# Top-k attention with a highway layer: earlier small top-eights, a reduction of its own for row maxima, one exponential a pair

## The chip, the cores and the metric

The kernel runs on one core of a Trainium2 chip. The metric is the device time of one execution in microseconds. TensorE (PE) does matmuls into PSUM, VectorE (DVE) and ScalarE (ACT) read PSUM and SBUF, GpSimd (POOL) works on SBUF, and the queues of SyncE (SP), ScalarE and GpSimd issue DMAs. Each engine takes its instructions in the order in which they were written; between engines, semaphores order the work.

## The reference

Attention over 8 batches, 8 heads, 576 rows and a head width of 64 keeps the 32 largest scores of each row; then a highway layer runs over the 4608 x 512 result.

```
scores = scale * np.matmul(q, k.transpose(0, 1, 3, 2))
kth = np.partition(scores, -top_k, axis=-1)[..., -top_k:-top_k + 1]
scores = np.where(scores >= kth, scores, -1000000000.0)
scores = scores - np.max(scores, axis=-1, keepdims=True)
attn = np.exp(scores)
attn = attn / (np.sum(attn, axis=-1, keepdims=True) + 1e-09)
attn_out = np.matmul(attn, v)
...
H = np.maximum(x @ w_h, 0.0)
T = 1.0 / (1.0 + np.exp(-(x @ w_t + b_t)))
out = T * H + (1.0 - T) * x
```

## The kernel before

A unit is 128 rows of scores with 576 columns. For the first 512 rows of a batch a unit is one head and one of four row tiles; the last 64 rows (the remainder) of two heads share a unit. Units go in 144 pairs, 18 a batch: 16 of whole row tiles (two heads of the same rows) and 2 of remainders. A pair's scores fill three banks of PSUM: the first unit has columns 0 to 511 in bank 0 and its last 64 at the start of bank 1, the second has its first 64 at the end of bank 1 and the rest in bank 2. Two such tiles exist (`xs`), so the scores of pair i + 2 can begin when pair i is read for the last time.

The order of all work is written by hand, in `step(i)`; 143 steps and `begin` and `finish` make the program. For pair i + 1 a step does the search for the threshold, for pair i the rest:

- PE adds the masks of pair i to its scores (`mask_add`, line 411), multiplies the weights of pair i - 3 by the values (line 501), runs filler matmuls (`spare`, line 279), then the scores of pair i + 2 (lines 310 and 319, for remainders 327 and 336), then a piece of the highway layer (line 529) or a transpose of later inputs.
- VectorE finds the eight largest of each of six segments of 96 columns of both units of pair i + 1 (`segments`, line 354, twelve instructions), then the eight largest scores below the threshold of pair i (`below`, line 424). Then comes `refine(i + 1)`: it merges the segments' eights (lines 367 to 377) and combines them (line 379, written into column 1 of the candidates). Line 383 reduces columns 0 and 1 of the candidates to each row's maximum and its threshold (the 24th or so largest score). In between stand `hits` and `pick_b` (lines 430 and 443), which pick the exact 32nd largest of pair i, and, in some steps, a reciprocal for the softmax's denominators (line 566). Last, `keep_both` (line 463) takes the minimum of the exponentials and of a 0-or-huge mask of pair i - 1. It is split in two, the first 64 columns of each unit before line 383 and the rest behind it, where no reciprocal stands in the step and both units are done alike; else it is one instruction or, in a few steps, two of another form (lines 457 and 466).
- ScalarE makes the mask of pair i - 1 (`above`, line 446), an evacuation of an earlier piece, the exponential of the first unit of pair i (`expo`, line 416), the copy of both units' scores of pair i + 1 into SBUF (line 349), perhaps another evacuation, the exponential of the second unit, and the sign masks of pair i + 1 with their counts (line 398), which wait for line 383.
- GpSimd compares the second unit with its threshold (line 449), does the additions and multiplications of the highway layer (lines 571, 617, 618, 631), `pick_a` (line 440) and `biases` (line 392), and issues DMAs. `biases` is made to wait for the last minimum.

Each row has its own maximum, taken off in the exponential through its bias. `wall` holds, for each unit, the maximum, the list that begins with the threshold, and the 32nd largest score. SP transposes the kept weights by DMA for the values' matmuls.

`finish` ends the last two pairs, checks that the search was exact for all rows (`sure`, line 948; a slow loop repeats the work otherwise) and stores the last rows.

Of the kernel before, what the change touches and what calls it, by code (L numbers as in the profile page):

```python
# [26 lines left out]
def kernel(  # L27
# [71 lines left out]
    TOP, THR, KTH = 0, 1, NPK + 1  # L99
    wall = consts.tile([P, NU + 2, NPK + 2], FP32)  # L100
    fac = consts.tile([P, 2, 2], FP32)
    nc.vector.memset(fac[:, :, 0], -scale)
    nc.vector.memset(fac[:, :, 1], -BIGK * (1.0 - 2.0**-24))
    be = consts.tile([P, NG + 1, 2, 2], FP32)
# [7 lines left out]
    eps = consts.tile([P, H], FP32)  # L112
    nc.vector.memset(eps[:], 2.0e-9)
    nc.vector.memset(wall[:, 0:2, KTH : KTH + 1], 0.0)

    def kth(u):
        return wall[:, u + 2, KTH : KTH + 1]

    def tb(u):
        return be[:, u // 2, u % 2, 0:1]  # L120

    def eb(u):
        return be[:, u // 2 + 1, u % 2, 1:2]

    cands = []
    for i in range(4):
        cand = consts.tile([P, 2, 8, 8], FP32, name=f"cand{i}")
        nc.vector.memset(cand[:, :, NSEG:, 0:1], -3.0e38)
        cands.append(cand)
# [167 lines left out]
    def scores(pair, prep):  # L297
# [5 lines left out]
        MB = 2 * BANK  # L303
        RA, RB = BANK, 2 * BANK - rem
        if qt < nfull:
            hp = heads2[0][0] // 2
            for n0 in range(0, MAIN, 256):
                for s, mo in ((0, 0), (1, MB)):
                    r = s * D
                    nc.tensor.matmul(  # L310
# [6 lines left out]
                    )  # L317
            ends = ps[:, BANK:MB].rearrange("p (a n) -> p a n", n=rem)[:, 0 :: BANK // rem - 1, :]
            nc.tensor.matmul(  # L319
                ends, qT[:, hp, qs : qs + P], kd[:, hp, :], start=True, stop=True  # L320
            )
        else:
            for (mo, ro), hh in zip(((0, RA), (MB, RB)), heads2):
                hp = hh[0] // 2
                for n0 in range(0, MAIN, 256):
                    for r in (0, D):
                        nc.tensor.matmul(  # L327
# [6 lines left out]
                        )  # L334
                for r in (0, D):
                    nc.tensor.matmul(  # L336
# [6 lines left out]
                    )  # L343
        both = bass.AP(tensor=ps.tensor, offset=ps[:].offset, ap=[ps[:].ap[0], [3 * BANK - S, 2], [1, S]])
        return ps[:, 0:S], ps[:, 3 * BANK - S : 3 * BANK], both

    def copy_scores(both):
        sc = scpool.tile([P, 2, S], FP32, name="sc")
        nc.scalar.copy(sc[:], both)  # L349
        return [sc[:, s, :] for s in range(2)]  # L350

    def segments(cand, sc, lo, hi):
        for s in range(lo, hi):
            nc.vector.max(cand[:, s, :], sc[:, s * SEG : (s + 1) * SEG])  # L354
# [4 lines left out]
    def refine(g, cand):  # L359
        u0, u1 = pairs[g][0], pairs[g][1] + 1  # L360
# [15 lines left out]
        for s in range(2):  # L376
# [6 lines left out]
        nc.vector.tensor_reduce(  # L383
            wall[:, u0:u1, TOP : THR + 1],
            cand[:, :, :, 0:2].rearrange("p s r k -> p s k r"),
            mybir.AxisListType.X,
            ALU.max,
        )
        yield

    def biases(g):
        return nc.gpsimd.tensor_tensor(be[:, g], wall[:, 2 * g : 2 * g + 2, TOP : KTH + 1 : KTH - TOP], fac[:], ALU.mult)  # L392

    def mask_count(u, ps):
# [5 lines left out]
            bias=wall[:, u, THR : THR + 1],  # L402
# [15 lines left out]

    def pair_tile(name):
# [3 lines left out]
    def below(u, ps):  # L423
        nc.vector.max(wall[:, u, THR + 1 : KTH], ps)  # L424
# [13 lines left out]
    def pick_a(pair, hit):  # L438
        u0, u1 = pair[0], pair[1] + 1
        nc.gpsimd.tensor_tensor(hit[:], hit[:], wall[:, u0:u1, THR:KTH], ALU.mult)  # L440

    def pick_b(pair, hit):
        nc.vector.tensor_reduce(wall[:, pair[0] + 2 : pair[0] + 4, KTH], hit[:], mybir.AxisListType.X, ALU.add)
# [15 lines left out]
    def keep_both(u, e, r, c0, c1):  # L459
# [3 lines left out]
        return nc.vector.tensor_tensor(out[:, :, c0:c1], e[:, :, c0:c1], r[:, :, c0:c1], ALU.min)  # L463
# [92 lines left out]
    def ffn_pieces(b, qt, xs):  # L556
# [4 lines left out]
        def norm():  # L561
            xs3 = xs[:, 0 : nh * DE].rearrange("p (h e) -> p h e", e=DE)
            rinv = cpool.tile([P, H], FP32, name="rinv")
            nc.gpsimd.tensor_tensor(rinv[:, 0:nh], xs3[:, :, D], eps[:, 0:nh], ALU.add)
# [18 lines left out]
            yield True  # L583
# [571 lines left out]
```

## Time and profile before

| | |
|---|---|
| median of 3 runs | 799.22 us (799.0 to 799.35) |
| the profiled execution | 800.24 us, its span 798.6 us |
| VectorE busy | 768.6 us |
| ScalarE busy | 756.8 us |
| TensorE busy | 692.5 us |
| GpSimd busy | 564.9 us |
| mean granted clock of TensorE | 0.996 |

A group line of the profile shows line, engine, operation, output and inputs with their shapes, the count, then busy time in us and the mean length of one in ns, then the idle time ahead of the group and what ended it. A timeline line shows start and length in us. A wait shows who waited for whom, the total in us, how often and the longest. A line by stretches shows the stretch, its length, and for each engine the busy time and the instructions in it, then TensorE's granted clock, the DMA engines' busy share and GB/s. In the chain's shares, an engine's name with q is its queue.

### The profile page before, as it was taken

The numbers are of one execution on the slowest core, as the hardware profiler recorded it, in microseconds if no ns is written. First come the engines' busy times: TensorE is split into PE (matmuls) and PEld (weight loads), VectorE is DVE, ScalarE is ACT, GpSimd is POOL, SyncE is SP. The second block draws the span as 40 slices with busy tenths as digits, with TensorE's granted clock in tenths as the row PEclk, the third lists the DMA queues.
The fourth block names the chain that finished last, engine by engine and source line by source line (L and its number), as shares of the span: only waits on it lengthen the run. The fifth ranks groups of instructions, "written<-read, shape, count | busy, mean of one in ns | idle before, by whom it ended". The sixth has DMA issues, their size and how long they took to land.

```text
span 798.6 us, 20350 instructions
## 1 busy us (share of the span) xinstructions
PE 692.5 (87%) x6459; PEld 494.4 (62%) x6459; DVE 768.6 (96%) x3947; ACT 756.8 (95%) x1401; POOL 564.9 (71%) x750
## 2 busy tenths in 40 slices
PE   7889998888988888888997889889898888988884
PEld 5666766666666666566665656656666666666552
DVE  6999999999999999999999999999999999999996
ACT  5999999999999999999999999999999999999984
POOL 2666867777777777787777876778777787676760
PEclk9999999999999999999999999999999999999998
DMA  6699967976799667987589766898677985565653
GB/s 123 87 132 167 133 121 138 155 130 94 137 156 151 109 97 134 157 143 117 98 147 164 125 112 111 154 149 129 109 128 141 166 117 100 96 110 100 114 85 89
DMA packets 341780, 100.32 MB, mean 126 GB/s; under 512 B 326048, under 2 KB 333856, under 8 KB 341664
## 3 DMA queue, kind: packets, MB, share of 16 engines
q1 hardware_dynamic: 286448, 79.14, 52.3%
q0 software_dynamic: 53536, 19.34, 22.4%
q8 instruction: 53, 0.87, 0.5%
q10 hardware_dynamic: 1680, 0.46, 0.3%
q14 instruction: 63, 0.52, 0.2%
HBM read 31.72 MB, written 9.44 MB: 52 GB/s over the span
## 4 chain that ended last, share of the span: by engine, by line
DVE 50%; ACT 29%; PE 14%; DMA 3%; issue 2%; SPq 1%; DVEq 0%; ACTq 0%
DVE cand L354 19%; DVE wall L424 14%; ACT m L398 8%; ACT e L416 7%; DVE ep L463 6%; ACT sc L349 6%; PE xs L327 4%; ACT r L446 3%; PE fp L529 2%; PE pso L279 2%; DMA xT<-xb 2%; PE xs L310 2%; ACT xs L515 1%; DVE en L374 1%; PE xs L411 1%
## 5 line engine op out<-in xcount | busy, mean ns | idle before, releaser
L354 DVE MAX8 cand<-xs 128x8 f32<-128x96 f32 x1728 | 298.6, 250 | 10.7 <-PE xs L336 7.0
L279 PE MATMUL pso<-cst,ident_b 128*128 128x252 bf16 x1841 | 247.0, 272 | 41.7 <-ACT xs L515 39.7
L449 POOL TENSOR_SCALAR r<-sc,wall 128x576 bf16<-128x576 f32 x135 | 232.5, 1722 | 0.0
L416 ACT ACTIVATE e<-sc,be 128x576 bf16<-128x576 f32 x288 | 227.9, 792 | 0.1
L279 PEld LDWEIGHTS <-ident_b 128*128 128x128 bf16 x1841 | 173.5, 98 | 80.7 <-issue 48.8
L424 DVE MAX8 wall<-xs 128x8 f32<-128x576 f32 x288 | 204.4, 751 | 4.5 <-PE xs L411 3.2
L310 PE MATMUL xs<-kT,qT 64*128 64x256 f32 x1024 | 145.3, 400 | 36.1 <-DVE high L367 29.7
L349 ACT COPY sc<-xs 128x1152 f32<-128x1152 f32 x144 | 161.6, 1122 | 1.0 <-DVE cand L354 0.9
L310 PEld LDWEIGHTS xs<-kT,qT 64*128 64x128 f32 x1024 | 93.1, 186 | 67.7 <-issue 40.3
L398 ACT ACTIVATE m<-xs,wall 128x576 int8<-128x576 f32 x144 | 107.9, 750 | 10.6 <-DVE wall L383 9.5
L463 DVE TENSOR_TENSOR ep<-e,r 128x1024 bf16<-128x1024 bf16 (+2 forms) x236 | 116.4, 493 | 0.3 <-issue 0.2
L440 POOL TENSOR_TENSOR hit<-hit,wall 128x18 f32<-128x18 f32 x143 | 32.2, 225 | 115.8 <-DVE hit L430 115.8
L398 ACT ACTIVATE m<-sc,wall 128x576 int8<-128x576 f32 x144 | 112.3, 780 | 0.0
L411 PE MATMUL xs<-m,ident_b 128*128 128x512 bf16 (+1 forms) x576 | 104.5, 285 | 9.0 <-ACT m L398 6.8
L446 ACT ACTIVATE r<-sc,be 128x576 bf16<-128x576 f32 x143 | 110.8, 775 | 0.0
L501 PEld LDWEIGHTS <-et 128*128 128x128 bf16 (+1 forms) x1600 | 68.6, 100 | 19.9 <-issue 3.5
L392 POOL TENSOR_TENSOR be<-wall,fac 128x4 f32<-128x4 f32 x144 | 29.1, 202 | 72.5 <-DVE ep L463 52.0
L501 PE MATMUL pso<-vb,et 128*128 128x65 bf16 (+1 forms) x1600 | 74.4, 194 | 1.1 <-DMA et<-ep 1.1
L411 PEld LDWEIGHTS <-ident_b 128*128 128x128 bf16 x576 | 51.0, 97 | 35.1 <-issue 13.8
L319 PEld LDWEIGHTS xs<-kd,qT 128*128 128x128 f32 x256 | 38.1, 188 | 42.5 <-issue 42.1
L319 PE MATMUL xs<-kd,qT 128*128 128x128 f32 x256 | 62.5, 326 | 0.0
L617 POOL TENSOR_TENSOR s<-h,x 128x512 f32<-128x512 f32 (+1 forms) x37 | 42.8, 1157 | 1.0 <-ACT h L616 1.0
(128 smaller groups left out, 999.6 us busy)
## 6 DMA issues: line engine op xcount, KB each, us to landing
kin<-in_k_dram SPq DMA_DIRECT2D x64, 128.0 KB, 3.2
qin<-in_q_dram SPq DMA_DIRECT2D x62, 128.0 KB, 3.2
out_dram<-s SPq DMA_DIRECT2D x30, 256.0 KB, 3.2
s<-h POOLq DMA_DIRECT2D x29, 256.0 KB, 3.9
xb<-x POOLq DMA_DIRECT2D x30, 128.0 KB, 2.8
vb<-in_v_dram POOLq DMA_DIRECT2D x28, 128.0 KB, 3.9
et<-ep SPq DMA_TRANSPOSE x143, 4.0
vb<-in_v_dram POOLq DMA_DIRECT2D x24, 64.0 KB, 3.1
```

The lines of the kernel that those rows point to most:

```text
L279: nc.tensor.matmul(po["t"][:, 4 * DE : BANK], ident_b[:], cst[:, 0 : BANK - 4 * DE], start=True, stop=True, skip_group_check=True,)
L310: nc.tensor.matmul(ps[:, mo + n0 : mo + n0 + 256], qT[r : r + D, hp, qs : qs + P], kT[r : r + D, hp, n0 : n0 + 256], start=(n0 == 0), stop ...
L349: nc.scalar.copy(sc[:], both)
L354: nc.vector.max(cand[:, s, :], sc[:, s * SEG : (s + 1) * SEG])
L398: nc.scalar.activation(m1[:].bitcast(I8)[:, 1 : 2 * S : 2], ps, AF.Sign, bias=wall[:, u, THR : THR + 1], scale=ABOVE, accum_out=csum[:, u ...
L411: nc.tensor.matmul(ps[:, s0:s1], ident_b[:], m1[:, s0:s1], start=False, stop=True, skip_group_check=True)
L416: nc.scalar.activation(e, sc, AF.Exp, bias=tb(u), scale=scale)
L424: nc.vector.max(wall[:, u, THR + 1 : KTH], ps)
L446: nc.scalar.activation(r, sc, AF.Relu, bias=eb(u), scale=BIGK)
L449: nc.gpsimd.tensor_scalar(r, sc, kth(u), None, ALU.is_ge)
L463: return nc.vector.tensor_tensor(out[:, :, c0:c1], e[:, :, c0:c1], r[:, :, c0:c1], ALU.min)
L501: nc.tensor.matmul(pso[r0 : r0 + ql, col : col + DE], ets[s][:, c, gi * P2 : gi * P2 + ql], vb[:, h, vc, :], start=(c == 0), stop=(c == nc ...
```

## The change

Three things are changed.

1. The matmuls of a pair's scores that write outside bank 0 are collected in `rest`, and the first unit's segments that lie wholly in bank 0 (five of six) are declared independent of them.
2. `refine` has two reductions in place of one. The first takes, over column 0 of the candidates of both units and with a padding in front and behind, the maximum of the first unit, of both units together, and of the second. The second takes the threshold of each unit from column 1.
3. For a pair of whole row tiles (128 of 144), one exponential covers both units, with the joint maximum of the pair; it stands where the first unit's stood, ahead of the score copy. The minimum of `keep_both` is always one instruction. Since the joint maximum is not each row's own, the small number added to a row's sum in the denominator is scaled: GpSimd subtracts the maxima of four pairs (`distances`) after `pick_a`, and ScalarE takes an exponential of 8 values a row (`expo_share`) in the next step, ahead of the copy of the attention output. A remainder pair keeps its two exponentials and has one more GpSimd instruction for their biases. The final check has a fourth part, that no row's maximum is too far below the joint one.

```
         for s, mo in ((0, 0), (1, MB)):
-            nc.tensor.matmul(
+            mm = nc.tensor.matmul(
...
+            if s:
+                rest.append(mm)
-    nc.tensor.matmul(ends, ...)
+    rest.append(nc.tensor.matmul(ends, ...))

-    def segments(cand, sc, lo, hi):
+    def segments(cand, sc, lo, hi, rest=()):
         for s in range(lo, hi):
-            nc.vector.max(cand[:, s, :], sc[:, s * SEG : (s + 1) * SEG])
+            ins = nc.vector.max(cand[:, s, :], sc[:, s * SEG : (s + 1) * SEG])
+            if (s + 1) * SEG <= BANK:
+                for mm in rest:
+                    tc.declare_no_dep(ins.ins, mm.ins, reason="another bank")

     # refine, behind the combination into cand[:, :, :, 1]
-        nc.vector.tensor_reduce(
-            wall[:, u0:u1, TOP : THR + 1],
-            cand[:, :, :, 0:2].rearrange("p s r k -> p s k r"),
-            mybir.AxisListType.X,
-            ALU.max,
-        )
+        at = cands4[:]
+        heads = bass.AP(tensor=at.tensor, offset=at.offset, ap=[at.ap[0], [64, 3], [64, 2], [8, NSEG]])
+        nc.vector.tensor_reduce(wall[:, g, 0:LIST], heads, mybir.AxisListType.XY, ALU.max)
+        yield
+        nc.vector.tensor_reduce(lists(g)[:, :, 0], cand[:, :, :, 1], mybir.AxisListType.X, ALU.max)
         yield

+    def biases(g):
+        if not joint(g):
+            nc.gpsimd.tensor_tensor(bs[:, g % 4], wall[:, g, 0:LIST:2], fat[:], ALU.mult)
+        return nc.gpsimd.tensor_tensor(be[:, g], wall[:, g, PEAK : KTH + LW + 1 : LW], fac[:], ALU.mult)

+    def distances(g):
+        g0 = g + 1 - NP
+        nc.gpsimd.tensor_tensor(dist[:, g0 : g + 1], wall[:, g0 : g + 1, 0:LIST:2],
+            wall[:, g0 : g + 1, PEAK].unsqueeze(2).to_broadcast([P, NP, 2]), ALU.subtract)
...
+            nc.scalar.activation(share[:], dist[...], AF.Exp, bias=eps[:, 0:1], scale=scale)

+    def exponentials(g):
+        e = pair_tile("e")
+        sc = st[g]["sc"]
+        if joint(g):
+            nc.scalar.activation(e[2][:], sc[2], AF.Exp, bias=be[:, g, 0:1], scale=scale)
+        else:
+            for s, u in enumerate(pairs[g]):
+                expo(u, sc[s], e[s])
+        return e

     # step
-            expo(pr[0], st[i]["sc"][0], st[i]["e"][0])
+            st[i]["e"] = exponentials(i)
         if nxt:
             copy_both(i + 1)
...
-            expo(pr[1], st[i]["sc"][1], st[i]["e"][1])
...
-        first = 0
-        if prev and ps_["one"] and not busy:
-            first = 64
-            keep_both(pu[0], ps_["e"][2], ps_["r"][2], 0, first)
         for _ in ra:
             pass
         last = masked()

     # finish
+        sure(3, dist[:], 1.0)
...
-        nc.vector.scalar_tensor_tensor(cond[:], wall[:, 0:NU, THR + 1], ABOVE, wall[:, 0:NU, THR], ALU.mult, ALU.add)
+        for s in range(2):
+            c = LIST + s * LW
+            nc.vector.scalar_tensor_tensor(
+                cond[:, s::2], wall[:, 0:NG, c + 1], ABOVE, wall[:, 0:NG, c], ALU.mult, ALU.add)
```

`wall` now has one row a pair, with three maxima in front of two lists, and the candidates of a pair have a column of padding on both sides; the other changes follow from that.

More of the change, by code (lines that the diff above doesn't have):

```diff
@@ L554, with denominators, ffn_pieces @@
     blocks = []
-    def ffn_pieces(b, qt, xs):
+    def denominators(e, rinv, sums, share):
+        if share is None:
+            return e.tensor_scalar(rinv, sums, 2.0e-9, None, ALU.add)
+        return e.tensor_tensor(rinv, sums, share[:], ALU.add)
+    def ffn_pieces(b, qt, xs, share=None):
         nh, ng, w = shape_of(qt)
@@ L563, in norm @@
             rinv = cpool.tile([P, H], FP32, name="rinv")
-            nc.gpsimd.tensor_tensor(rinv[:, 0:nh], xs3[:, :, D], eps[:, 0:nh], ALU.add)
+            denominators(nc.gpsimd, rinv[:, 0:nh], xs3[:, :, D], share)
             yield
@@ L651, in blk_norm @@
         rinv = cpool.tile([P, H], FP32, name="rinv")
-        nc.vector.tensor_tensor(rinv[:, 0:nh], xs3[:, :, D], eps[:, 0:nh], ALU.add)
+        denominators(nc.vector, rinv[:, 0:nh], xs3[:, :, D], k["share"])
         nc.vector.reciprocal(rinv[:, 0:nh], rinv[:, 0:nh])
```

145 lines of the change are left out of this document (92 added, 53 removed).

## The prediction

> **What bounds the kernel now.** I read the busy line of the page and the chain's shares first, then busy time in three stretches, then the waits, then VectorE's instructions in order of time.
>
> ```profile
> PE 692.5 (87%) x6459; PEld 494.4 (62%) x6459; DVE 768.6 (96%) x3947; ACT 756.8 (95%) x1401; POOL 564.9 (71%) x750
> ...
> DVE 50%; ACT 29%; PE 14%; DMA 3%; issue 2%; SPq 1%; DVEq 0%; ACTq 0%
> ```
>
> VectorE (DVE) and ScalarE (ACT) are both nearly full, and the chain changes between them and TensorE (PE). So I asked by stretch, with PE's busy time first, then its loads, VectorE, ScalarE, GpSimd:
>
> ```profile
> 378.85:388.90 10.05, 9.95 (x100) 6.94 (x101) 9.13 (x52) 9.77 (x18) 7.58 (x11) 1.00 0.59 105
> 72.00:103.00 31.00, 28.64 (x278) 21.20 (x277) 29.54 (x150) 30.22 (x57) 25.50 (x31) 1.00 0.98 133
> 399.55:430.00 30.45, 26.96 (x256) 19.29 (x253) 30.45 (x159) 29.97 (x56) 23.13 (x31) 1.00 0.86 152
> ```
>
> The third is the common case: VectorE is busy for all 30.45 us. In the second, in the first batch, ScalarE is the fuller one. The first covers the two steps of a batch whose scores are of the remainder rows (line 327): PE works 9.95 of 10.05 us, and VectorE has 0.9 us to spare. There are eight such stretches, one a batch. Which waits VectorE has:
>
> ```profile
> DVE cand L354 <- PE xs L336: 7.0, 15, 0.5
> DVE wall L424 <- PE xs L411: 3.2, 5, 1.1
> DVE cand L354 <- PE xs L319: 3.0, 7, 0.6
> PEld L529 <- DMA xT<-xb: 3.9, 4, 1.4
> PE xs L411 <- ACT m L398: 6.8, 24, 0.7
> ACT m L398 <- DVE wall L383: 9.5, 25, 0.9
> ```
>
> All that waiting is some 13 us. This is the most that better waits can return; any instruction added to VectorE costs in full wherever VectorE is the bound.
>
> **The change, part by part.**
>
> **The five small top-eights (line 354).** They will wait for the matmuls of the first bank alone; the sixth and the second unit's wait for the rest. Five of them give PE 0.8 us more, by the row of twelve in 2.07 us below, and the longest wait is 0.6, so the wait at line 354 should vanish. But who is late next? In the remainder steps (the 15 waits on line 336) the next thing VectorE needs is the mask matmuls of line 411, and they stand on PE behind the same scores, in a stretch where PE has 0.10 us of idle time. There the wait moves to line 424. I take 0.05 us a stretch, 0.4 us in all (0 to 0.8, all the idle time). The waits on line 319 are outside: 3.0 us, to which comes the overlap of 85 ns worked out below that each of the seven also loses, 3.6 in all. Behind them stands the wait for masks at line 424, so not everything counts: I take 2.8 (1.0 to 3.6).
>
> **Row maxima by their own instruction, and the joint minimum whole.** Here are a step whose minimum is split and one whose isn't, from the last combination of the refinement to the next top-eights:
>
> ```profile
> 401.77 0.19 DVE L379 SCALAR_TENSOR_TENSOR cand<-en 128x16 f32<-128x16 f32 x1
> 401.86 0.20 DVE L566 RECIPROCAL rinv<-rinv 128x8 f32<-128x8 f32 x1
> ...
> 402.00 0.21 DVE L383 TENSOR_REDUCE wall<-cand 128x4 f32<-128x32 f32 x1
> 402.12 0.75 DVE L463 TENSOR_TENSOR ep<-e,r 128x1152 bf16<-128x1152 bf16 x1
> ...
> 402.79 2.07 DVE L354 MAX8 cand<-xs 128x8 f32<-128x96 f32 x12
> ...
> 406.58 0.23 POOL L440 TENSOR_TENSOR hit<-hit,wall 128x18 f32<-128x18 f32 x1 [0.48 <-DVE hit L430]
> ...
> 406.98 0.19 DVE L379 SCALAR_TENSOR_TENSOR cand<-en 128x16 f32<-128x16 f32 x1
> 407.07 0.22 DVE L463 TENSOR_TENSOR ep<-e,r 128x128 bf16<-128x128 bf16 x1
> 407.21 0.21 DVE L383 TENSOR_REDUCE wall<-cand 128x4 f32<-128x32 f32 x1
> 407.34 0.68 DVE L463 TENSOR_TENSOR ep<-e,r 128x1024 bf16<-128x1024 bf16 x1
> ...
> 407.94 2.07 DVE L354 MAX8 cand<-xs 128x8 f32<-128x96 f32 x12
> ```
>
> ```profile
> L354 DVE MAX8 cand<-xs 128x8 f32<-128x96 f32 x1728 | 298.6, 250 | 10.7 <-PE xs L336 7.0 <-PE xs L319 3.0
> L383 DVE TENSOR_REDUCE wall<-cand 128x4 f32<-128x32 f32 x144 | 29.9, 208 | 0.2
> L443 DVE TENSOR_REDUCE wall<-hit 128x2 f32<-128x18 f32 x144 | 22.4, 156 | 0.0
> L463 DVE TENSOR_TENSOR ep<-e,r 128x128 bf16<-128x128 bf16 x101 | 22.1, 219 | 0.2 <-issue 0.2
> L566 DVE RECIPROCAL rinv<-rinv 128x8 f32<-128x8 f32 x31 | 6.1, 195 | 0.0
> L566 DVE RECIPROCAL rinv<-rinv 128x4 f32<-128x4 f32 x7 | 1.2, 170 | 0.0
> ```
>
> Instructions overlap: twelve of 250 ns would be 3.00 us and take 2.07, so each starts (3.00 - 2.07)/11 = 85 ns before the one ahead ends. From start to start, the split step spends 0.09 + 0.14 + 0.13 + 0.60 = 0.96 us here, the whole one with a reciprocal 0.09 + 0.14 + 0.12 + 0.67 = 1.02. In both the reduction starts 0.23 after the combination it depends on, whatever lies between.
>
> The new reduction of the maxima reads 36 elements, nearly what line 383 reads (32), with the same stride: 213 ns, or 0.13 from start to start. It doesn't need the combination, so it takes the place of the small minimum as filler. The second reduction reads 16 elements: between line 443 (18 dense elements, 156 ns) and line 383 (208 ns) lies 0.07 to 0.12 a start; I take 0.09, nearer to the first by size, with a little for the stride. A split step becomes 0.09 + 0.13 + 0.09 + 0.67 = 0.98, 0.025 more. A step with a reciprocal becomes 0.09 + 0.11 (195 less 85) + 0.13 + 0.09 + 0.67 = 1.09, 0.07 more.
>
> 101 steps are split and 38 (31 + 7) have a reciprocal; eight of each lie in the PE stretches, which cover the cost. 93 x 0.025 + 30 x 0.07 = 4.4 us, of which I give 0.5 back for other steps that wait at line 424 anyway: 3.9. The low end is line 443's price for both, held by the 0.23: +0.01 and nothing, 0.9 us. The high end is line 383's price for both: 0.06 and 0.11, 9 us.
>
> [...]
>
> **One exponential a pair.** ScalarE's slope and overlap:
>
> ```profile
> 400.07 0.78 ACT L416 ACTIVATE e<-sc,be 128x576 bf16<-128x576 f32 x1
> ...
> 400.74 1.11 ACT L349 COPY sc<-xs 128x1152 f32<-128x1152 f32 x1
> ```
>
> ```profile
> L416 ACT ACTIVATE e<-sc,be 128x576 bf16<-128x576 f32 x288 | 227.9, 792 | 0.1
> L349 ACT COPY sc<-xs 128x1152 f32<-128x1152 f32 x144 | 161.6, 1122 | 1.0 <-DVE cand L354 0.9
> L252 ACT COPY kT<-fp 128x512 f32<-128x512 f32 x31 | 18.2, 588 | 0.0
> ```
>
> An element costs (1122 - 588)/640 = 0.83 ns, so a joint exponential should take 792 + 576 x 0.83 = 1.27 us. Two take 1.58 less one overlap of 0.11 (0.78 - 0.67): 0.2 us less, in 128 of 144 pairs, 26 us of ScalarE's time (0 if it grew in proportion). Most of this is idle time to be: the masks wait for line 383 on VectorE 25 times already. It pays where PE waits for masks and VectorE for PE. Line 424's waits on 411 are 3.2 us, but four of its five I put down to the four late transposing DMAs before line 529, which stay. I take 1.0 (0 to 2.0), with what it adds in the first batch. The order also moves: the score copy and the evacuation after it come some 0.48 later (1.15 for the joint one against 0.67 start to start), hidden by the masks, which still come after; if that cover went, PE would wait for the evacuation before line 529.
>
> ```profile
> POOL hit L440 <- DVE hit L430: 115.8, 143, 3.7
> ```
>
> **Small additions.** 32 tiny exponentials for the denominators on ScalarE, ahead of the copy that PE's fillers wait for, 32 subtractions on GpSimd after line 440, one more check and two halves for one at the end: 0.3 us (0 to 1.5); the first are paid by the 26 us above, the subtractions fit into GpSimd's wait of 115.8 us.
>
> **The sum** against the profiled execution (800.24 us, span 798.6; 1.02 above the median of 799.22): -0.4 - 2.8 + 3.9 - 1.0 + 0.3 = 0.0. So 799.2 for the median: the waits that go pay for the instruction that comes.
>
> **The rivals.**
>
> The waits go and the reductions are cheap: line 443's price (0.9 us) and the gains near their ends (-0.8 - 3.6 - 1.5): -4.7 with the additions, 794.5. For it: VectorE's waits are real, and the filler hides in the 0.23. Against it: line 383 has the stride of both.
>
> The reductions decide, and the time is slower: with line 383's price on both (9 us, 8.5 after what is covered) and gains of 4.2 and 0.3 of additions it is 803.8. Place: between lines 379 and 463, in the stretches where VectorE is 100% busy. It decides once the two add over 0.034 us a step (4.2 / 123), which is 0.23 us for both in a split step (0.96 - 0.09 - 0.67 + 0.034). Against it: 16 elements should not cost what 32 do.
>
> GpSimd's subtraction blocks VectorE. [...]
>
> ```profile
> 281.73 1.27 POOL L617 TENSOR_TENSOR s<-h,x 128x512 f32<-128x512 f32 x1 [0.58 <-ACT h L616]
> ...
> 282.40 0.66 DVE L367 TENSOR_TENSOR high<-cand 128x48 f32<-128x48 f32 x1
> ```
>
> Line 367 took 0.66 us here for 48 elements and ended 0.06 behind GpSimd's instruction. The subtraction stands behind line 440 (406.58 to 406.81 above); at line 440's own length it would run to 407.04, and the combination starts at 406.98. If each is hit by a whole subtraction, 32 x 0.2 = 6.4 us: 805.6; the point from which it decides is the 0.06 of overlap just worked out, 1.9 us. [...]
>
> The change doesn't act: the top-eights' wait passes to line 424 everywhere and the masks come no sooner: 799.2 + 3.9 + 0.3 = 803.4, on the slower side too.
>
> **How the numbers follow.** No change is what lies within 0.2%, 1.6 us. The sum has 0.38 (its own range 797 to 801.4; a tenth of all falls below 797.6 and 0.02 above 800.8, the rest, 0.26, is no change). Cheap reductions: 0.25. Dear reductions: 0.24, a blocked VectorE 0.06, a wait that only moves 0.07. Faster 0.35, same 0.26, slower 0.39. With 794 to 804.5 the range leaves out about 2 in 10, the far ends of the cheap case and of the blocked one.
>
> **What would show it.** Line 354 has hardly any idle time before it, while line 424's wait on line 411 grows by about 0.5 us in each remainder stretch, whose length stays 10.0. The two reductions take some 213 and 172 ns. The joint exponential takes 1.27 us; ScalarE's busy share falls to about 92%, and its masks wait more often for VectorE. VectorE stays at 96% or above. It is wrong if the remainder stretches get shorter, if a reduction takes over 250 ns, or if line 379's successor or the `high` line stretches.

## The result, and the profile after

| | before | after |
|---|---|---|
| median of 20 runs each, side by side | 799.61 us (798.9 to 801.29) | 801.32 us (799.79 to 802.82) |
| ratio, 95% interval | | 1.0020 (1.0013 to 1.0026) |
| the profiled execution, its span | 800.24, 798.6 us | 801.33, 799.7 us |

The change makes the kernel 1.7 us slower. The forecast was no change, 799.2 us. The time lies within the stated range, but the interval of the ratio leaves out 1: the kernel moved, and the sum said that it would not. The changed kernel's line numbers are its own: 354 became 375, 424 became 487, 411 became 464, 383 became 410 (maxima) and 412 (thresholds), 463 became 526, 529 became 592.

The page of the changed kernel, busy times and the chain's shares:

```profile
PE 690.8 (86%) x6461; PEld 493.8 (62%) x6461; DVE 771.5 (96%) x3993; ACT 741.7 (93%) x1307; POOL 578.4 (72%) x799
...
DVE 75%; PE 13%; ACT 6%; issue 3%; DMA 2%; SPq 0%; POOL 0%; DVEq 0%; ACTq 0%; POOLq 0%
```

ScalarE is relieved by 15 us and hardly on the chain any more (29% before); VectorE has 75% of it (50% before). The program's end now hangs on VectorE, and on what makes VectorE wait. Groups of instructions, each with what ended the idle time ahead of it:

```profile
L375 DVE MAX8 cand<-xs 128x8 f32<-128x96 f32 x1728 | 298.0, 252 | 0.8 <-PE xs L328 0.7
L487 DVE MAX8 wall<-xs 128x8 f32<-128x576 f32 x288 | 205.1, 756 | 13.1 <-PE xs L464 12.0
L476 ACT ACTIVATE e<-sc,be 128x1152 bf16<-128x1152 f32 x128 | 161.0, 1257 | 0.1
```

```profile
L410 DVE TENSOR_REDUCE wall<-cand 128x3 f32<-128x36 f32 x144 | 28.6, 199 | 0.0
L436 ACT ACTIVATE share<-dist,eps 128x8 f32<-128x8 f32 x32 | 9.5, 297 | 0.0
L412 DVE TENSOR_REDUCE wall<-cand 128x2 f32<-128x16 f32 x144 | 25.9, 180 | 0.0
L622 POOL TENSOR_SCALAR rinv<-xs 128x4 f32<-128x4 f32 x7 | 1.6, 230 | 0.6
```

The idle time of 10.7 us ahead of the small top-eights is gone, and that ahead of line 487 is 13.1 where 4.5 stood: of 9.9 us taken there 8.6 turn up here, though not all for this reason, as the runs below show. In the steps of remainder rows it moved whole. Here is one of their eight stretches before (VectorE in order of time), then after:

```profile
377.38 1.41 DVE L424 MAX8 wall<-xs 128x8 f32<-128x576 f32 x2
381.07 2.08 DVE L354 MAX8 cand<-xs 128x8 f32<-128x96 f32 x12 [0.39 <-PE xs L336]
383.06 1.41 DVE L424 MAX8 wall<-xs 128x8 f32<-128x576 f32 x2
386.83 2.08 DVE L354 MAX8 cand<-xs 128x8 f32<-128x96 f32 x12 [0.54 <-PE xs L336]
389.01 1.43 DVE L424 MAX8 wall<-xs 128x8 f32<-128x576 f32 x2
```

```profile
375.71 1.42 DVE L487 MAX8 wall<-xs 128x8 f32<-128x576 f32 x2
378.96 2.06 DVE L375 MAX8 cand<-xs 128x8 f32<-128x96 f32 x12
381.35 1.43 DVE L487 MAX8 wall<-xs 128x8 f32<-128x576 f32 x2 [0.32 <-PE xs L464]
384.56 2.07 DVE L375 MAX8 cand<-xs 128x8 f32<-128x96 f32 x12
387.32 1.43 DVE L487 MAX8 wall<-xs 128x8 f32<-128x576 f32 x2 [0.69 <-PE xs L464]
```

The two steps took 389.01 - 377.38 = 11.63 us and take 387.32 - 375.71 = 11.61. The waits of 0.39 and 0.54 stand now as 0.32 and 0.69 before the masks' matmuls.

The two reductions, in a step with a reciprocal and in one without:

```profile
399.96 0.19 DVE L404 SCALAR_TENSOR_TENSOR cand<-en 128x16 f32<-128x16 f32 x1
400.05 0.20 DVE L635 RECIPROCAL rinv<-rinv 128x8 f32<-128x8 f32 x1
400.16 0.17 DVE L410 TENSOR_REDUCE wall<-cand 128x3 f32<-128x36 f32 x1
400.24 0.17 DVE L412 TENSOR_REDUCE wall<-cand 128x2 f32<-128x16 f32 x1
400.33 0.75 DVE L526 TENSOR_TENSOR ep<-e,r 128x1152 bf16<-128x1152 bf16 x1
401.00 2.07 DVE L375 MAX8 cand<-xs 128x8 f32<-128x96 f32 x12
404.08 1.43 DVE L487 MAX8 wall<-xs 128x8 f32<-128x576 f32 x2 [1.01 <-PE xs L464]
...
406.30 0.19 DVE L404 SCALAR_TENSOR_TENSOR cand<-en 128x16 f32<-128x16 f32 x1
406.39 0.21 DVE L410 TENSOR_REDUCE wall<-cand 128x3 f32<-128x36 f32 x1
406.52 0.18 DVE L412 TENSOR_REDUCE wall<-cand 128x2 f32<-128x16 f32 x1
406.62 0.75 DVE L526 TENSOR_TENSOR ep<-e,r 128x1152 bf16<-128x1152 bf16 x1
407.28 2.07 DVE L375 MAX8 cand<-xs 128x8 f32<-128x96 f32 x12
```

The step without takes 407.28 - 406.30 = 0.98 from the combination to the next top-eights (0.96 before, 0.98 forecast), the one with takes 1.04 (1.02 before, 1.09 forecast). Over all such steps of the two traces the medians are 0.986 and 0.949 without, 1.040 and 1.015 with. Between the two shown stands a wait of 1.01 us at line 487, which the kernel before did not have in this step (step 73 as counted below). What TensorE was late for there is told by the view of one tile, `xT`, which the transposing DMAs write and line 592 reads. Before, then after; the numbers behind a name are us and times:

```profile
  DMA xT<-xb: 7.1, 8
...
  PEld L529: 4.5, 5
...
DMA to landing us min/median/max: 2.4/2.8/4.8
```

```profile
  DMA xT<-xb: 9.4, 8
...
  PEld L592: 6.1, 6
...
DMA to landing us min/median/max: 2.3/2.9/5.5
```

Both kernels wait for these transfers; the changed one waits longer. Whether that is part of the change's price, and what the rest is, the runs had to tell.

### The profile page after: what moved, and what is told of

Same layout as the page of the kernel before. It is cut to its first block, busy times and chain, and to the rows that moved or that the text cites. A ratio compares the mean times of both kernels' runs of the same rounds, so it can differ in the third digit from the quotient of the medians.

```text
span 799.7 us, 20355 instructions
## 1 busy us (share of the span) xinstructions
PE 690.8 (86%) x6461; PEld 493.8 (62%) x6461; DVE 771.5 (96%) x3993; ACT 741.7 (93%) x1307; POOL 578.4 (72%) x799
## 4 chain that ended last, share of the span: by engine, by line
DVE 75%; PE 13%; ACT 6%; issue 3%; DMA 2%; SPq 0%; POOL 0%; DVEq 0%; ACTq 0%; POOLq 0%
DVE cand L375 26%; DVE wall L487 22%; DVE ep L526 9%; PE xs L345 4%; PE fp L592 3%; DVE en L399 2%; DVE en L402 2%; PE pso L296 2%; DVE cand L404 2%; DVE high L392 2%; DMA xT<-xb 2%; ACT m L451 2%; DVE low L394 2%; PE xs L464 1%; DVE neg L396 1%
## 5 line engine op out<-in xcount | busy, mean ns | idle before, releaser
L487 DVE MAX8 wall<-xs 128x8 f32<-128x576 f32 x288 | 205.1, 756 | 13.1 <-PE xs L464 12.0
L476 ACT ACTIVATE e<-sc,be 128x1152 bf16<-128x1152 f32 x128 | 161.0, 1257 | 0.1
L451 ACT ACTIVATE m<-xs,wall 128x576 int8<-128x576 f32 x144 | 107.5, 747 | 28.4 <-DVE wall L412 27.2
L464 PE MATMUL xs<-m,ident_b 128*128 128x512 bf16 (+1 forms) x576 | 102.7, 285 | 4.6 <-ACT m L451 2.8
L526 DVE TENSOR_TENSOR ep<-e,r 128x1152 bf16<-128x1152 bf16 x135 | 101.0, 748 | 0.5 <-issue 0.5
L422 POOL TENSOR_TENSOR be<-wall,fac 128x3 f32<-128x3 f32 x144 | 28.4, 197 | 66.0 <-DVE ep L526 47.7
L687 POOL TENSOR_TENSOR h<-h,x 128x512 f32<-128x512 f32 (+1 forms) x37 | 43.0, 1162 | 0.6
```

The source lines that it names most:

```text
L451: nc.scalar.activation(m1[:].bitcast(I8)[:, 1 : 2 * S : 2], ps, AF.Sign, bias=top9(u, 0, 1), scale=ABOVE, accum_out=csum[:, u : u + 1],)
L464: nc.tensor.matmul(ps[:, s0:s1], ident_b[:], m1[:, s0:s1], start=False, stop=True, skip_group_check=True)
L476: nc.scalar.activation(e[2][:], sc[2], AF.Exp, bias=be[:, g, 0:1], scale=scale)
L487: nc.vector.max(top9(u, 1), ps)
L526: return nc.vector.tensor_tensor(out, e[:], r[:], ALU.min)
```

## The experiments

Every run has the kernel before beside it, and is given as a ratio to it with its 95% interval; 0.1% is 0.8 us. Steps are counted so that step n runs from VectorE's line 424 (487) for pair n - 1 to the one for pair n.

### One part at a time, on the kernels as they are

Run e1_bank_only: the first edit alone, on the kernel before.

```
-            segments(st[g]["cand"][:, s], st[g]["ps"][s], k, k + 1)
+            segments(st[g]["cand"][:, s], st[g]["ps"][s], k, k + 1, () if s else st[g]["ps"][3])
```

> The kernel before with the first edit alone: the five small top-eights wait only for the bank they read. Theory (the removed wait mostly reappears at line 424's wait, so the edit is worth little): the idle time in front of line 354 falls from 10.7 us to under 1 us, the idle time in front of line 424 grows by 5 to 9 us, and the time is 0.5 to 2.5 us under before, 797.1 to 799.1 on a before of 799.6. Rival (the edit acts freely and the reductions eat its gain): 4 to 6 us under before. Rival (the edit does nothing): within 0.4 us of before.

797.7 us, ratio 0.9970 (0.9958 to 0.9981): 2.4 us gained. The idle time ahead of the top-eights went to 0.4 us, that ahead of the next line grew to 14.0.

Run e2_no_bank: the changed kernel without the first edit.

```
-            segments(st[g]["cand"][:, 1 + s], st[g]["ps"][s], k, k + 1, () if s else st[g]["ps"][3])
+            segments(st[g]["cand"][:, 1 + s], st[g]["ps"][s], k, k + 1)
```

> The kernel after with the first edit undone: the five small top-eights wait again for the matmuls as the tracker sets it. Theory: idle time in front of the top-eights' line comes back (5 to 10 us), the wait of the line that writes over the scores falls by 4 to 8 us, and the time is 0.5 to 2.5 us above after, 801.8 to 803.8 on an after of 801.3. Rival (the edit was worth 4 us or more and only hidden by the reductions): 805 or more. Rival (without its wait VectorE only runs into GpSimd's hold and into later transfers, so the edit loses): 800.3 or less.

804.35 us, ratio 1.0049 (1.0036 to 1.0062), 2.3 us above the changed kernel by the ratios, 3.0 by the medians. The first edit is worth about the same in both. So the loss comes from the other two.

Run e3_share_behind: the small exponential behind the copy of the attention output.

```
-        while lows:
-            lows.pop(0)()
         if back:
             back_pv(j)
             back_xs(j)
             st.pop(j)
+        while lows:
+            lows.pop(0)()
```

> The kernel after with the remainder's exponential issued behind ScalarE's copy of the output instead of ahead of it. Theory (the exponential ahead of the copy delays TensorE's filler work and the masks behind it): the steps that carry it, three of them at 0.14 us more than before, go back, and the time falls by 0.3 to 1.0 us, to 800.3 to 801.0 on an after of 801.3. Rival (it lies beside other work): within 0.3 us of after. Rival (the remainder's subtraction on GpSimd now gets its operand later and holds the steps behind it): above after by 0.5 us or more.

801.95 us, ratio 1.0023 (1.0014 to 1.0031): no gain to be seen. In the trace the three steps did go back from 5.32 to 5.18 us; the runs spread from 799.97 to 802.98, and 0.4 us drowns in that. The theory held in the step and could not be told in the time.

Run e4_two_reductions: on the kernel before, two reductions and the minimum always whole. Both reductions read 16 elements here; the changed kernel's first reads 36.

```
-        nc.vector.tensor_reduce(wall[:, u0:u1, TOP : THR + 1],
-            cand[:, :, :, 0:2].rearrange("p s r k -> p s k r"), mybir.AxisListType.X, ALU.max)
+        nc.vector.tensor_reduce(wall[:, u0:u1, TOP], cand[:, :, :, 0], mybir.AxisListType.X, ALU.max)
+        yield
+        nc.vector.tensor_reduce(wall[:, u0:u1, THR], cand[:, :, :, 1], mybir.AxisListType.X, ALU.max)
...
-        if prev and ps_["one"] and not busy:
-            first = 64
-            keep_both(pu[0], ps_["e"][2], ps_["r"][2], 0, first)
```

> The kernel before with the reduction over 36 maxima replaced by two over 16 each, into the lists of maxima and thresholds, and the joint minimum always as one instruction; exponentials and waits as before. Theory (two reductions cost about 0.03 us a step of two forms and 0.02 to 0.1 us a step with a reciprocal, plus what the whole minimum opens): 2.5 to 5 us above before, 802.1 to 804.6 on a before of 799.6. Rival (the reductions are cheap, and the loss sits in the late transfers or the exponentials): within 1 us of before. Rival (dear): 6 us or more above before.

801.62 us, ratio 1.0024 (1.0015 to 1.0033), 1.9 us above: less than the theory gave. With the first edit's 2.4 taken off, the changed kernel should then be 0.5 us faster than before; so some 2 us were in the joint exponential, where I had forecast a gain, or in something that comes with it.

### Which part of the rest?

Run e5_no_share leaves out the distances and small exponentials; every denominator adds the constant 2e-9.

```
-            share, ex = distances(g)
-            shares.append(share)
-            lows.append(ex)
+            shares.append(None)
```

> The kernel after without the remainder: the distances on GpSimd and the 32 small exponentials on ScalarE are left out and the denominators take the constant 2e-9, so what the joint exponential leaves below is not added. By the first four runs the joint exponential and what comes with it cost about 2.0 us on top of the reductions and the bank edit. Theory A (the remainder's work costs that: GpSimd's subtraction in front of the denominators, ScalarE's 32 exponentials): 1.2 to 2.2 us under after, 799.4 to 800.5 on an after of 801.6. Theory B (the late transposing transfers cost it): within 0.4 us of after. Theory C (the joint exponential of 1.26 us, twice as long as one, holds up ScalarE's copy, filter and masks): within 0.4 us of after.

803.33 us, ratio 1.0042 (1.0028 to 1.0056). None of the three had this: leaving work out cost 1.7 us or more. The reason came later (below, the add of an immediate).

Run e6_split_exp: two exponentials again, with the joint bias, the first unit's here and the second's at its old place.

```
...
-            nc.scalar.activation(e[2][:], sc[2], AF.Exp, bias=be[:, g, 0:1], scale=scale)
...
+            bias = be[:, g, 0:1] if joint(g) else tb(pairs[g][s])
+            nc.scalar.activation(e[s], st[g]["sc"][s], AF.Exp, bias=bias, scale=scale)
...
```

> The kernel after with the joint exponential as two again, at their two old places, with the joint bias. Theory C (one exponential of 1.26 us is what costs): 1 to 2 us under after, 799.6 to 800.6. Theory A (the remainder's work) and theory B (late transfers): ScalarE gets its 0.2 us a pair back, 26 us in all, and the time is 0.3 to 2 us above after, 801.9 to 803.6.

802.73 us, ratio 1.0037 (1.0023 to 1.0051). Theory C falls: the joint exponential does not cost, the two cost more.

Run e7_after_early_xT: the transposing transfer one step earlier on SP, its readers where they were.

```
-            turns.append((i + 2, casts.pop(0)()))
+            turns.append((i + 1, casts.pop(0)()))
...
-            ready.extend([hh, tt])
+            return [hh, tt]
...
+        while landing and landing[0][0] <= i:
+            ready.extend(landing.pop(0)[1])
         while turns and turns[0][0] <= i and len(flying) < 2:
-            turns.pop(0)[1]()
+            landing.append((i + 1, turns.pop(0)[1]()))
```

> The kernel after with each transposing transfer issued one step (5 us) earlier, the projections that read it staying where they are. Theory B (the late transfers, 4 waits of 5.1 us in all in front of line 592, are what costs): those waits vanish, and the time falls by 2 to 4 us, 797.6 to 799.6. Theories A and C: the waits vanish, but what the same edit takes off the kernel with the bank edit alone (4 waits of 4.4 us) is as much, so that the distance between the two stays at 4 us. Rival (the transfers collide elsewhere, or TensorE catches up anyway): within 0.5 us of after.

797.22 us (796.9 to 797.37), ratio 0.9966 (0.9952 to 0.9979): 4.1 us under the changed kernel, and the spread of the runs fell from 3 us (20 runs) to half a us (5 runs). In the view of `xT` the line of waits for the DMA is gone:

```profile
  ACT xT L735: 1.6, 4
...
  PEld L592: 1.0, 2
...
DMA to landing us min/median/max: 2.5/3.0/4.7
```

Run e8_bank_early_xT: the first edit and the same earlier transfers on the kernel before.

> The kernel before with the bank edit and the same earlier transfers: a candidate for a version faster than both. Theory B: 1 to 2 us under the bank edit alone (797.7), and so the distance to the run with the changed kernel falls from 4 to 2 us. Theories A and C: 2 to 3.5 us under it, 794.2 to 795.7, the distance stays. Rival (the waits were covered): within 0.5 us of 797.7.

794.44 us (794.07 to 794.55), ratio 0.9930 (0.9916 to 0.9944): faster than both kernels, by 5.6 us than before. The distance to the changed kernel shrank from 3.6 us (801.32 - 797.7) to 2.8, between the 2 of theory B and the 4 of A and C; the time itself lies where A and C had it, so this run alone does not decide.

### The parts again, with the transfers out of the way

With the earlier transfers, smaller differences can be read. Runs that were not made side by side still differ by chance: the kernel before, run beside each group, had medians from 799.49 to 800.09. A difference of under half a us between medians of two groups is therefore not told apart from nothing. Run f4_before_early has them on the kernel before, f1_bank_early_two_red adds the diff of e4 to e8, f2_early_no_share is e5 and f3_early_split_exp is e6 with the earlier transfers.

> The kernel before with the earlier transfers alone. Theory (the waits for the late transfers were the same in both kernels but for 1 us, which went against the changed one): 796.3 to 797.2, so that the whole change then comes out within 1 us of no change, and the bank edit at 1.9 to 2.8 us. Rival (the waits of before were covered): 798.5 or more.

796.98 us, ratio 0.9961 (0.9947 to 0.9975). So with the transfers early the whole change moves the time from 796.98 to 797.22, by 0.24 us (0.4 by the ratios), which is not told apart from nothing. Of the 1.7 us, 1.2 to 1.5 are the transfers. The two profiled executions say the same step by step: in the changed kernel step 73 is 1.12 us longer and step 79 0.80, step 133 is 0.52 shorter and step 97 0.25. Each of the four waits for such a transfer in at least one of the two kernels, and together they make 1.15 us; the spans differ by 1.1.

> The kernel before with the bank edit, the earlier transfers, the two reductions over 16 and the minimum always whole; exponentials as before. Between 794.44 (without the reductions) and 797.22 (the whole change), both with the earlier transfers. Theory (the reductions cost what the prediction gave them, and little of it is covered): 797.0 to 798.5, so that the joint exponential gains up to 1 us. Rival (the reductions cost about 1.7 us as on the kernel before, and the joint exponential with its remainder costs the rest): 795.8 to 796.6.

796.06 us, ratio 0.9950 (0.9936 to 0.9963): the rival was right, two reductions over 16 elements with the whole minimum cost 1.6 us (796.06 - 794.44).

> The changed kernel with the earlier transfers and without the remainder (distances and small exponentials left out, the denominators take the constant). The late transfers gone, theory A (GpSimd's subtraction in front of the denominators and the small exponentials cost 0.12 us in two steps of each tile of rows, which would be 0.12 x 14): 795.3 to 796.3, 1 to 2 us under 797.22. Rival (leaving it out cost 1.7 us on the changed kernel, and only the late transfers made that): as theory A. Rival (it lies beside other work): within 0.4 us of 797.22.

799.46 us, ratio 0.9994 (0.9985 to 1.0003): 2.2 us above e7, again slower without the work, and now without the transfers to blame. Against e7, 22 of its steps with a reciprocal are 0.1 to 0.13 us longer each. Its groups show why, first GpSimd's adds for the denominators before the change, then in f2:

```profile
L564 POOL TENSOR_TENSOR rinv<-xs,eps 128x8 f32<-128x8 f32 x31 | 6.3, 204 | 0.0
L564 POOL TENSOR_TENSOR rinv<-xs,eps 128x4 f32<-128x4 f32 x7 | 1.4, 200 | 0.0
```

```profile
L620 POOL TENSOR_SCALAR rinv<-xs 128x8 f32<-128x8 f32 x31 | 7.7, 249 | 2.8
L620 POOL TENSOR_SCALAR rinv<-xs 128x4 f32<-128x4 f32 x7 | 1.6, 235 | 0.6
```

The add of an immediate took 249 ns where that of a tile took 204, and started 2.8/31 = 0.09 us late. VectorE's reciprocal reads the result. The changed kernel has seven of these adds, in the remainder rows (line 622 above), and behind them the reciprocal starts 0.18 us after the combination, where it was 0.09 before the change. This was in the diff, in `denominators`, and I had not priced it.

> The changed kernel with the earlier transfers and two exponentials of 0.79 us a pair in place of one of 1.26. Theory (the relief of ScalarE is worth something in the first batch alone): 0.5 to 1.5 us above 797.22, 797.7 to 798.7. Rival (the long exponential holds up the copy and the masks behind it): 0.5 us or more under 797.22. Rival (off the path): within 0.4 us.

798.92 us, ratio 0.9988 (0.9979 to 0.9997): one exponential instead of two gains 1.7 us, more than the 0.5 to 1.5 expected. The expectation put the gain into the first batch; of 2.0 us that the steps of the two traces differ, 1.4 lie behind it.

Run g4_early_floor: e7 with a tile in place of the immediate.

```
-        return e.tensor_scalar(rinv, sums, 2.0e-9, None, ALU.add)
+        return e.tensor_tensor(rinv, sums, floor[:, 0 : sums.shape[1]], ALU.add)
```

> The changed kernel with the earlier transfers; the denominators of the remainder rows add a tile that holds 2e-9, as the kernel before does, in place of an immediate. Theory (GpSimd's add of an immediate starts 0.09 us late and takes 0.235 us against 0.20, VectorE's reciprocal waits 0.085 us for it, and the steps of 31 such adds were 0.12 us longer each where all of them were so): the 7 steps lose 0.12 us each, 796.2 to 796.6 on 797.22. Rival (off the path): within 0.3 us of 797.22.

796.27 us, ratio 0.9957 (0.9943 to 0.9970): 0.95 us gained for seven instructions, by medians of two groups (0.7 by the ratios). In the traces five of the seven steps are 0.09 to 0.11 shorter, 0.5 us; the rest of the 0.95 is not accounted for.

Run h1_floor_no_share is g4 without the distances and small exponentials.

> The changed kernel with the earlier transfers, without the remainder's distances and exponentials, and with the constant of the denominators from a tile in place of an immediate everywhere. Theory (leaving the remainder out cost time above only because 31 more adds took the immediate, 0.12 us a step each; the remainder itself costs 0.14 us in three steps and little else): 795.5 to 796.2, so 0.1 to 0.8 us under the 796.27 with the remainder and 3 us or more under the 799.46 with the immediate. Rival (the immediate isn't it): 798.5 or more.

795.83 us, ratio 0.9950 (0.9937 to 0.9964): the remainder's work costs 0.44 us, and in the traces it is three steps (81, 99 and 117) of 0.14 to 0.15 each; the immediate in all 38 adds cost 3.6 (799.46 - 795.83).

Run h2_bank_early_whole_min is e8 with the minimum always whole.

> The kernel before with the bank edit, the earlier transfers and the joint minimum always whole, one reduction as before. Between 794.44 (split minimum) and 796.06 (whole minimum and two reductions). Theory (in a split step the small minimum fills the 0.23 us that the reduction must wait for the combination; whole, the step is 0.06 us longer, in 93 steps, and the second reduction in its place gives 0.03 of it back): 798 to 800. Rival (the whole minimum saves an instruction and costs nothing): 794.0 to 794.8.

798.15 us, ratio 0.9980 (0.9971 to 0.9989). The whole minimum alone costs 3.7 us, and the second reduction in its place gives 2.1 of them back. VectorE in a step without a reciprocal, and the group of the reduction:

```profile
405.18 0.19 DVE L386 SCALAR_TENSOR_TENSOR cand<-en 128x16 f32<-128x16 f32 x1
405.40 0.21 DVE L390 TENSOR_REDUCE wall<-cand 128x4 f32<-128x32 f32 x1
405.53 0.75 DVE L470 TENSOR_TENSOR ep<-e,r 128x1152 bf16<-128x1152 bf16 x1
```

```profile
L390 DVE TENSOR_REDUCE wall<-cand 128x4 f32<-128x32 f32 x144 | 30.4, 211 | 3.6
```

With nothing between, the reduction still starts 0.22 us after the combination, and VectorE idles, 3.6 us in all ahead of this line. From the combination to the next top-eights such a step takes 0.95 us in e8, 1.02 here and 0.99 in f1. So something useful should stand in that time; the reduction of the maxima gives back about half of what the 64 columns of the minimum had hidden.

These runs make a chain from the kernel before to the changed one, both with early transfers:

| step | us | difference |
|---|---|---|
| before (f4) | 796.98 | |
| first edit (e8) | 794.44 | -2.54 |
| minimum whole (h2) | 798.15 | +3.71 |
| second reduction (f1) | 796.06 | -2.09 |
| joint exponential, its biases, the reduction over 36 (h1) | 795.83 | -0.23 |
| distances and small exponentials (g4) | 796.27 | +0.44 |
| immediate in seven denominators (e7) | 797.22 | +0.95 |

The 143 steps of the profiled executions together give -2.3, +4.0, -2.4, -0.3, +0.7 and +0.6 us for the same edits. So the large ones are sure, and the small ones good to some 0.3 us.

### Why the transfers came later

In the changed kernel the transfer issued in step 78 lands 5.5 us after its issue, before the change 4.7. The DMA view of that stretch, from issue to landing, shows queues with their packets and share of 16 engines, then the transfer. Before:

```profile
q8 instruction: 1, 0.02, 1.5%
...
xT<-xb SPq DMA_TRANSPOSE x1, 4.7
```

After:

```profile
q14 instruction: 1, 0.01, 1.9%
q8 instruction: 1, 0.02, 1.1%
...
xT<-xb SPq DMA_TRANSPOSE x1, 5.5
```

There is a packet of queue 14, which the profile calls an instruction packet and which I take for a piece of an engine's code: 1.9% of 16 engines for 5.6 us is 1.7 us on one DMA engine. Such a piece recurs every 4.4 steps, some 122 of VectorE's instructions; before the change it came in step 80, when the transfer had landed. VectorE had begun 2203 instructions when it came before the change and 2206 in the changed kernel, so in these two its place went by VectorE's count. The change gives VectorE 46 instructions more, and each piece comes a little earlier in the steps. If the piece makes the transfer late, instructions that do nothing should do the same. Runs g1_after_pad27, g2_before_pad25 and g3_before_early_pad25 add 27, 25 and 25 memsets of one element to the changed kernel, the kernel before and f4, where VectorE idles at the start:

```
+    spacer = consts.tile([P, 1], FP32)
+    for _ in range(25):
+        nc.vector.memset(spacer[:], 0.0)
```

> The kernel before with 25 such memsets at the same place: its code fetch of step 80 moves to where the changed kernel has it, about 2 us into step 79. Theory F: the transfer of step 78 lands at 5.2 us or more (4.7 in the profile of before), and the time rises by 0.6 to 1.5 us, 800.6 to 801.5 on a before of 799.95. Rival: within 0.4 us of before.

802.8 us (801.04 to 804.59), ratio 1.0038 (1.0027 to 1.0049): 3.0 us slower, twice the 0.6 to 1.5 expected and more than the change itself, by instructions without work. In the two traces step 79 is 1.83 us longer than before the change, step 73 1.05 and step 97 0.72. The DMA view of the same stretch, and the view of `xT`:

```profile
q14 instruction: 1, 0.01, 2.1%
q8 instruction: 1, 0.02, 1.3%
...
xT<-xb SPq DMA_TRANSPOSE x1, 5.4
```

```profile
  DMA xT<-xb: 11.1, 8
...
  PEld L532: 6.5, 5
```

> The kernel before with the earlier transfers and the same 25 memsets, the control: no projection waits for a transfer there. Theory F: within 0.3 us of 796.98. Rival (memsets or fetches cost time by themselves): 0.5 us or more above.

796.81 us, ratio 0.9965 (0.9951 to 0.9979), as f4: without the late transfers the memsets cost nothing.

> The changed kernel with 27 one-element memsets added on VectorE at 3.2 us, where it idles until 7.3 us. They do no work; they move each later fetch of VectorE's code (8 KB, queue 14) about one step earlier, so that the one at 2.0 us into step 79, 1.7 us long, no longer falls beside the transposing transfer of step 78. Theory F (that fetch makes this transfer land at 5.5 us after its issue and not at 4.7): landing at 4.9 or less, the wait at step 79 at 1.5 us or less (2.0 in the changed kernel's profile), and the time 0.6 to 1.5 us down, 800.1 to 801.0 on 801.6. Rival (the landing comes from the transfers themselves): landing 5.2 or more, and within 0.4 us of 801.6.

801.97 us, ratio 1.0026 (1.0017 to 1.0036): half a miss. In its trace the piece of code came before the transfer, which landed 4.9 us after its issue, and VectorE's wait at the end of step 79 fell from 1.92 us to 1.28; the time did not fall. Other waits for transfers stayed or grew (six in front of line 595 with 5.3 us in all, against four with 5.1). The profiled execution, the longest of the ten, shows one more thing: its 143 steps together are 0.9 us shorter than the changed kernel's, as the theory had it, but the program's end, behind them, is 2.0 us longer. There VectorE waits 2.73 us at line 625 where it waited 0.80, and from 786 to 788 us the granted clock of TensorE was 0.50 where it was 1.00. Whether the other nine runs lost their time in the same place is not known.

So it is shown that the transfers cost the time, and that empty instructions move it by microseconds through them. That the piece of code is what delays the transfer is not shown. Over ten profiles of kernels with late transfers the transfer of step 78 landed after 5.2 to 5.6 us in the six where a piece came 1.7 to 2.0 us into step 79, and after 4.6 to 5.2 in the four where it came at another time. But in e7 and g3, where the transfer was out of the way, the piece in step 79 took 0.7 us: the two are slow together, and which holds the other is open. It also leaves out step 73, the larger part of the change's loss in the profiled pair. The transfer of step 72, for which that step waits, lands after 2.5 us or 4.6 to 4.7 from profile to profile (the longer in the changed kernel, e4, g1 and g2, 2.5 in the other six) for a reason that was not found.

## Why the prediction was wrong

**The step that failed** is half a sentence under the exponential: "the four late transposing DMAs before line 529, which stay". They were seen, and counted as a constant. They were taken as the cause of four of the five waits at line 424, rightly: with the earlier transfers (f4, 796.98 us against 799.85) these waits are gone. But they did not stay. They land so close to their reader that a later landing is a longer wait at once, and they took 1.2 to 1.5 of the 1.7 us: steps 73 and 79 grew by 1.12 and 0.80 us. Nothing in the sum or in the rivals had this mechanism. The view of `xT` before the change held a sign of it, a landing time of up to 4.8 us against a median of 2.8. Why each landed later in the changed kernel stays open.

**The rest of the sum came out, by errors that cancel.** Forecast 0.0, measured 0.24 us with the transfers out of the way. That is luck: the reductions cost 1.6 us less than forecast, the first edit gave 0.7 less and the additions cost 0.6 to 1.1 more. Term by term:

- The first edit: forecast -3.2, measured -2.5. The mechanism was right: nothing in the remainder stretches, whose length stayed (11.63 and 11.61 us), the gain elsewhere. The wait that moves there was forecast as 0.5 us a stretch and is 0.32 + 0.69.
- The reductions with the whole minimum: forecast +3.9, measured 1.6 in f1 with two reductions over 16. The changed kernel's first reads 36: a step with a reciprocal takes 1.040 us with it and 1.005 in f1, and 23 of these steps are 0.025 to 0.037 longer in h1 than in f1, 0.7 us. I estimate 2.3 us from both. The prices of a step were both off: 0.025 more was forecast without a reciprocal and 0.037 came out, 0.07 with one and 0.025 came out, since the second reduction starts 0.08 us after the first there, not 0.13. In the sum this cancels: 93 x 0.037 + 30 x 0.025 = 4.2 us, where 4.4 stood. So the mis-sized part is what lies beside other waits: 0.5 was given, and 1.9 is left over, which no run measured by itself. The two took 199 and 180 ns (213 and 172 forecast).
- One exponential a pair: its length was right (1.27 forecast, 1257 ns), as was ScalarE's share (92% and 93%), and its masks wait 27.2 us for VectorE (line 412) where 9.5 stood. Forecast -1.0; f3 shows -1.7 for the merging, but only -0.23 is left together with what comes along. Of the 1.5 between, 0.7 are the reduction over 36 above; the rest was not taken apart, and so small a rest is hardly told apart from chance between groups.
- Small additions: forecast +0.3, measured 0.44 for the remainder and 0.5 to 0.95 for the immediate. The second was missed altogether: "32 tiny exponentials", "32 subtractions" and "one more check" were listed, and the changed operation in `denominators` was not.

**The rivals.** Neither cheap nor dear reductions: 1.6 to 2.3 lies between the 0.9 of the one and the 9 of the other. GpSimd's subtraction did not block VectorE: the combination took 189 ns before and 188 after, the `high` line 205 and 210. The wait at line 375 did move, but not everywhere, or the first edit alone would have gained nothing.

## What to carry to other kernels

Before pricing a change on a full engine, look for transfers that land just as they are read, and issue them earlier first: here that was worth 2.9 us on the kernel before, against 1.7 for the whole change, and it turned a spread of 3 us into half a us on the changed kernel, so that single edits could be read. Price the operations a diff replaces, not only those it adds: seven small adds that took an immediate cost 0.5 to 0.95 us, since a full engine waited for them. A gap that a dependency leaves on a full engine is worth keeping filled: taking 64 columns of a minimum out of it cost 3.7 us here, and a reduction in their place gave 2.1 back.

## What the hardware showed that was not expected

The profile shows instruction packets beside the data's and gives their time as a share of the same 16 DMA engines (queues 8 and 14, 53 and 63 packets, 0.4% and 0.2% in the changed kernel). 25 empty memsets at the start made the kernel 3.0 us slower; with the transfers issued earlier the same memsets changed it by 0.2 us, which is nothing. That they act by moving these packets fits the traces and is not shown. In step 79 of the changed kernel the one wait of VectorE, 1.92 us, was for TensorE (line 464), and TensorE's longest, 2.3 us, for the transfer. The packet beside that transfer took 1.7 us, against 0.7 with the transfer out of the way; which of the 16 engines it was on, and whether it held the transfer up, is not known.

GpSimd's add of an immediate to 128x8 values took 249 ns and started 0.09 us late (f2); the add of two tiles took 204 and did not (the kernel before).
